# Batch 0 of a spectral filter and MLP kernel: two-bank products and evictions, tables inside the filter stage, filter halves copied within SBUF

## The chip, the cores and the metric

The kernel runs on one NeuronCore of a Trainium2 chip. The metric is the device time of one execution in microseconds (us), as the median of several runs. A profile, taken by the hardware profiler on one more execution, gives the span from the first to the last instruction; its span is some 1.8 us shorter than the device time of the same run. Engines are named as the profile names them: PE is TensorE's matmuls, PEld its weight loads, DVE is VectorE, ACT is ScalarE, POOL is GpSimd, SP is SyncE.

## The reference

```python
def _attn_ref(x, filt_r, filt_i):             # x: (8, 3008, 256)
    X = np.fft.rfft(x, axis=1)
    Y = X * (filt_r + 1j * filt_i)[None]      # filters: (1505, 256)
    return np.fft.irfft(Y, n=x.shape[1], axis=1)

def _moe_ref(x, w_in, w_out):                 # 24064 tokens, 256 -> 2048 -> 256
    h = x @ w_in
    g = 0.5 * h * (1.0 + erf(h / sqrt(2)))    # exact gelu
    return g @ w_out
```

The second function takes the first one's output, all batches in a row. All inputs and the output are float32; the kernel computes in bf16 with float32 sums.

## The kernel before

The Fourier transform of 3008 = 47 x 64 points is done as matmuls with small tables (T1 to T4). For batches 1 to 7 these matmuls are strewn among the MLP matmuls of the batch ahead. Batch 0 has nothing to hide behind: the MLP can't start before all of its output y is there, since its last step writes columns that are spread over the whole sequence. That path, and nothing else, is changed. Its stages are:

```python
    for k, n in ((0, 4), (4, 6), (10, 6), (16, 8)):
        m.load_filters(k, n)      # 4 parts of 8 DMAs: 2 tensors x 4 groups of 32 partitions;
                                  # groups 2 and 3 hold the same data as groups 0 and 1
    m.load_w_in()
    for u in range(16):
        m.c1(u // 2, u % 2)       # first transform of x
        ...
    m.load_x(1); m.load_w_out(0); m.load_w_out(8)
    m.tables_inverse()            # T4 and T3: matmuls, then evictions by DVE and ACT
    for p in range(14):
        if p < 12:
            m.c1t(p)              # transpose, evicted by ACT
        if 1 <= p < 13:
            m.c2(p - 1)           # second transform, times the filter on DVE
        ...
        if p in (3, 5, 7, 9, 11, 13):
            m.c3((p - 3) // 2)    # inverse; evicted by ACT into vt
    for u in range(20):           # last stage
        if u < 16:
            m.c3t(u)              # transposes of vt, evicted into d
        if u >= 3 and u % 2 == 1 and (u - 3) // 2 < 8:
            for h in range(2):
                m.s4(0, (u - 3) // 2, h, both=True)   # products with T4, evicted into y
```

```python
    def c2(self, p):              # before: two products of 512 columns from one PSUM bank each
        for t, o, n in ((p1, 1, 0), (p2, 0, 1)):
            ps = self.bank("ps_c2", True)
            ...                   # 2 matmuls
            nc.vector.tensor_tensor(out=t, in0=ps, op=ALU.mult, in1=self.F[:, n, 2*p:2*p+2, :]...)
```

The evictions of d and y alternate between ACT and DVE. F comes by Pool's DMA queue, which casts float32 to bf16 on the way; the framework lets at most eight of these DMAs be in flight.

## Time and profile before

| before | |
|---|---|
| device time, first three runs | 790.97, 791.30, 792.12 us |
| span of the profiled run | 790.6 us |
| granted TensorE clock | 0.999 |
| PE busy | 762.5 us, 96% |
| first filter product | 19.87 us |
| filter parts complete (0 to 3) | 17.1, 23.3, 29.4, 35.1 us |
| last filter product ends | 39.54 us |
| first MLP matmul (ps_h) | 50.20 us |
| from there to the end | 740.4 us |

The table is to be read from below. The last row is 94% of the span and is TensorE nearly without a gap, so only the 50.2 us above it can move by this change, and they are read from the waits of DVE, ACT and the DMA queue rather than from shares of busy time. The lines follow in the prediction.

### The profile page before, as it was taken

The page shows a single profiled execution, that of the slowest core. Times are in us where ns is not written, and L with a number is a line of the kernel's source. Part 1 is how long each engine was busy: PE and PEld are TensorE (multiplying, and loading weights), DVE is VectorE, ACT ScalarE, POOL GpSimd, SP SyncE. Part 2 cuts the span into 40 slices and gives each one's busy share as a digit, 9 for nine tenths or more (in the row PEclk, how much of TensorE's full clock was granted, in tenths as well). Part 3 has the DMA queues.
Part 4 walks back from the last instruction along what each step waited for, and adds up shares of the span by engine and source line. Part 5 has one row for each costly group of instructions (what it writes and reads, how often), then busy time and mean ns, then how long its engine had stood idle before and what let it go on. Part 6 is the DMA issues. An engine that isn't in the chain of part 4 may idle for free.

```text
span 790.6 us, 14618 instructions
## 1 busy us (share of the span) xinstructions
PE 762.5 (96%) x5817; PEld 539.1 (68%) x5914; DVE 407.6 (52%) x733; ACT 570.5 (72%) x982; POOL 65.3 (8%) x161
## 2 busy tenths in 40 slices
PE   4799999999999999999999999999999999999997
PEld 4556776677676767667677676667767767666666
DVE  7784756466464645646455564546645366411011
ACT  6688965798557885588755887569865688666663
POOL 8610200011000200002000010001100000000000
PEclk9999999999999999999999999999999999999999
DMA  8994862555435553446614566154642521401111
GB/s 128 178 161 132 158 161 68 147 119 114 114 84 155 104 135 84 109 139 130 145 50 109 148 119 157 40 160 108 125 130 65 162 78 58 133 31 38 41 41 54
DMA packets 88390, 87.21 MB, mean 110 GB/s; under 512 B 6081, under 2 KB 78273, under 8 KB 88321
## 3 DMA queue, kind: packets, MB, share of 16 engines
q1 hardware_dynamic: 77760, 68.70, 30.6%
q0 software_dynamic: 10560, 17.57, 15.5%
q8 instruction: 46, 0.75, 0.4%
q14 instruction: 24, 0.19, 0.1%
HBM read 57.15 MB, written 46.66 MB: 131 GB/s over the span
## 4 chain that ended last, share of the span: by engine, by line
PE 90%; DMA 5%; DVE 2%; POOL 1%; issue 1%; ACT 0%; SPq 0%; DVEq 0%; POOLq 0%
PE ps_o L420 41%; PE ps_h L406 37%; PE ps_s L231 3%; PE ps_s L306 3%; PE ps_s L278 2%; PE ps_s L254 2%; DMA d_sb<-R 1%; DMA F<-in_filt_i_dram 1%; DMA F<-in_filt_r_dram 1%; DMA x_sb<-in_x_dram 1%; DVE d_sb L218 1%; POOL x_sb L87 1%; POOL F L95 1%; DMA R<-a_sb 1%; DMA b_sb<-R 0%
## 5 line engine op out<-in xcount | busy, mean ns | idle before, releaser
L409 ACT ACTIVATE g_sb<-ps_h 128x512 bf16<-128x512 f32 x752 | 439.4, 597 | 189.1 <-PE ps_h L406 163.5
L420 PE MATMUL ps_o<-w_out_sb,g_sb 128*128 128x256 bf16 x3008 | 449.0, 272 | 3.0
L406 PE MATMUL ps_h<-y_sb,w_in_sb 128*128 128x512 bf16 (+2 forms) x1503 | 426.6, 365 | 0.2 <-ACT y_sb L216 0.2
L420 PEld LDWEIGHTS <-g_sb 128*128 128x128 bf16 x3008 | 287.6, 98 | 133.7
L406 PEld LDWEIGHTS <-w_in_sb 128*128 128x128 bf16 x1600 | 155.1, 98 | 23.0 <-issue 0.5
L424 DVE COPY ost<-ps_o 128x512 f32<-128x512 f32 x94 | 64.4, 685 | 125.1 <-PE ps_o L420 124.6
L261 DVE TENSOR_TENSOR p<-ps_s,F 128x512 bf16<-128x512 f32 x84 | 58.1, 692 | 103.8 <-ACT p L260 97.3
L220 DVE TENSOR_SCALAR y_sb<-ps_s 128x376 bf16<-128x376 f32 x120 | 65.3, 548 | 82.0 <-PE ps_s L306 81.9
L218 DVE CAST a_sb<-ps_s 96x512 bf16<-96x512 f32 x112 | 76.3, 685 | 40.5 <-PE ps_s L231 40.4
L218 DVE CAST v_sb<-ps_s 128x512 bf16<-128x512 f32 x84 | 57.6, 687 | 12.9 <-PE ps_s L278 12.7
L306 PEld LDWEIGHTS <-d_sb 96*128 96x128 bf16 x512 | 33.8, 97 | 30.2 <-issue 2.3
L259 ACT ACTIVATE p<-ps_s 64x512 bf16<-64x512 f32 x84 | 49.9, 594 | 2.2 <-ACT g_sb L409 0.2
L260 ACT CAST p<-ps_s 64x512 bf16<-64x512 f32 x84 | 48.5, 577 | 1.0
L100 POOL COPY gate<-p 1x1 bf16<-1x1 bf16 x48 | 8.5, 176 | 480.6 <-DVE p L263 480.6
L231 PE MATMUL ps_s<-x_sb,T 94*96 94x512 bf16 x112 | 42.6, 381 | 0.5
L306 PE MATMUL ps_s<-T,d_sb 96*128 96x94 bf16 x448 | 36.3, 204 | 2.6 <-DMA d_sb<-R 1.3
L263 DVE TENSOR_TENSOR p<-p,p 128x512 bf16<-128x512 bf16 x84 | 35.7, 425 | 2.9
L87 POOL DMA_DIRECT2D x_sb<-in_x_dram x64 | 33.9, 530 | 19.0 <-issue 11.1
L262 DVE TENSOR_TENSOR p<-p,F 128x512 bf16<-128x512 bf16 x84 | 34.9, 415 | 0.0
L254 PE MATMUL ps_s<-b_sb,T 128*128 128x256 bf16 x168 | 32.1, 273 | 0.3
L278 PE MATMUL ps_s<-p,T 128*128 128x256 bf16 x168 | 32.1, 273 | 0.3
L278 PEld LDWEIGHTS <-T 128*128 128x128 bf16 x168 | 16.4, 98 | 20.1 <-DVE p L263 0.5
(84 smaller groups left out, 189.0 us busy)
## 6 DMA issues: line engine op xcount, KB each, us to landing
out_dram<-ost SPq DMA_DIRECT2D x94, 256.0 KB, 2.5
x_sb<-in_x_dram POOLq DMA_DIRECT2D x64, 188.0 KB, 3.9
R<-a_sb SPq DMA_DIRECT2D x56, 192.0 KB, 3.0
b_sb<-R SPq DMA_DIRECT2D x28, 384.0 KB, 4.4
R<-v_sb SPq DMA_DIRECT2D x42, 256.0 KB, 4.0
d_sb<-R SPq DMA_DIRECT2D x56, 192.0 KB, 4.6
w_in_sb<-in_moe_w_in_dram POOLq DMA_DIRECT2D x2, 512.0 KB, 8.6
w_out_sb<-in_moe_w_out_dram POOLq DMA_DIRECT2D x2, 512.0 KB, 10.1
```

The costliest lines, as they stand in the source:

```text
L218: self.nc.vector.tensor_copy(out=out, in_=in_)
L220: self.nc.vector.tensor_scalar(out=out, in0=in_, scalar1=scale, scalar2=None, op0=ALU.mult)
L231: nc.tensor.matmul(ps[0:96, :], lhsT=self.T1, rhs=self.st[b, "x"][:, 2 * u:2 * u + 2, :], start=True, stop=True)
L259: nc.scalar.activation(out=p2[0:64], in_=ps[64:128], func=AF.Copy, scale=-1.0)
L260: nc.scalar.copy(out=p2[64:128], in_=ps[0:64])
L261: nc.vector.tensor_tensor(out=p1, in0=ps, in1=f(0), op=ALU.mult)
L278: nc.tensor.matmul(ps[:, 256 * i:256 * i + 256], lhsT=self.T3[:, k].rearrange("p a b -> p (a b)"), rhs=w[:, 256 * i:256 * i + 256], start= ...
L306: nc.tensor.matmul(ps[:, 94 * i:94 * i + 94], lhsT=d[:, (grp % 2) * 4 + i, 128 * half:128 * half + 128], rhs=t4, start=True, stop=True)
L406: nc.tensor.matmul(ps[:, o:o + n], lhsT=self.w_in_sb[:, dc, jc * 128:jc * 128 + 128], rhs=self.ring[:, dc, off:off + n], start=(dc == 0), ...
L409: nc.scalar.activation(out=self.st["g", t][:, jc, :], in_=ps, func=AF.Gelu)
L420: nc.tensor.matmul(ps[:, tile_i % 2, :], lhsT=g[:, jc, tile_i * 128:tile_i * 128 + 128], rhs=self.w_out_sb[:, jc, :], start=(jc == 0), sto ...
L424: nc.vector.tensor_copy(out=ost, in_=ps)
```

## The change

Its intent is a shorter front. A product with the filter covers two PSUM banks (1024 columns) and one DVE instruction instead of two; the transposes and inverses around it work two units ahead on single banks; T3 and T4 are made inside the filter stage instead of ahead of it; d and y are evicted two banks at a time; and of the last three filter parts only one half comes from HBM, the other, which holds the same data, is copied from it within SBUF, so that fewer DMAs with fewer small packets are needed. PSUM is divided into three sets of pools, one after the other.

```diff
-    for k, n in ((0, 4), (4, 6), (10, 6), (16, 8)):
-        m.load_filters(k, n)
+    m.load_filters(0, 4, 2)
+    m.load_filters(4, 6)
+    m.load_filters(10, 6)
+    m.dup_filters(4, 6)
+    m.load_filters(16, 8)
+    m.dup_filters(10, 6)
+    m.dup_filters(16, 8)
     m.load_w_in()
...
+    def dup_filters(self, k0, k):
+        self.nc.gpsimd.dma_start(out=self.F[64:128, :, k0:k0 + k, :], in_=self.F[0:64, :, k0:k0 + k, :])
...
-    m.tables_inverse()
-    for p in range(14):
...
+    for p in range(3):
+        m.c1t(p)
+    for q in range(7):
+        if q < 6:
+            m.c2(2 * q)
+            m.table_3(q)
+            if 2 * q + 3 < 12:
+                m.c1t(2 * q + 3)
+            m.c2(2 * q + 1)
+            if 2 * q + 4 < 12:
+                m.c1t(2 * q + 4)
+        if q == 4:
+            m.table_4()
+        if q >= 1:
+            m.c3(q - 1)
+    wide.close()
+    wide = ctx.enter_context(ExitStack())
+    m.psum(wide, v=(4, 2))
+    for u in range(10):
+        if u < 8:
+            m.c3t(u)              # 8 transposes, one eviction of 1024 columns
+        if u >= 2:
+            m.c4(u - 2)           # 8 products, one eviction of 752 columns
+    wide.close()
+    m.psum(ctx, h=(3, 1), o=(2, 1), f=(3, 1))
...
     # c2
+        ps = self.bank("ps_c2", "w")                 # [128, 2, 512]
         ...
+        nc.vector.tensor_tensor(out=w, in0=ps, op=ALU.mult,
+                                in1=self.F[:, :, 2 * p:2 * p + 2, :]...)
```

Cut: the table routines, the pool bookkeeping, a table load of ACT that comes earlier, and c1, whose first eight evictions are now all ACT's and its last eight all DVE's.

## The prediction

> **What bounds the kernel now.** I read the shares of the span, the chain that ended last in order of time, and then the DVE timeline of the stretch that the chain pointed to.
>
> ```profile
> PE 762.5 (96%) x5817; PEld 539.1 (68%) x5914; DVE 407.6 (52%) x733; ACT 570.5 (72%) x982; POOL 65.3 (8%) x161
> ...
> PE 90%; DMA 5%; DVE 2%; POOL 1%; issue 1%; ACT 0%; SPq 0%; DVEq 0%; POOLq 0%
> ```
>
> TensorE bounds the span: 90% of the chain. The other tenth is nearly all at the front, where batch 0 goes through its transform before the first matmul of the MLP (ps_h). In the chain in order of time (start, duration, what):
>
> ```profile
> 29.64 5.50 DMA F<-in_filt_i_dram
> ...
> 38.86 0.69 DVE p L352
> ...
> 39.97 1.08 ACT vt_sb L370 x2
> 41.05 0.05 issue
> 41.10 0.58 PE ps_c3t L383 x7
> ...
> 45.10 0.46 DVE y_sb L220
> 45.56 0.60 DVE d_sb L218
> ...
> 50.20 0.61 PE ps_h L406 x2
> ```
>
> The first ps_h starts at 50.20; from there the chain is TensorE almost without a break. So the change, which touches batch 0 alone, is worth what it moves that 50.20 by, at most a few per cent of 790.6. Two stretches decide it. Up to 39.55 DVE multiplies with the filters and waits for them:
>
> ```profile
> 19.87 3.08 DVE L352 TENSOR_TENSOR p<-ps_c,F 128x512 bf16<-128x512 f32 x5 [0.58 <-DMA F<-in_filt_r_dram]
> 23.39 3.08 DVE L352 TENSOR_TENSOR p<-ps_c,F 128x512 bf16<-128x512 f32 x5 [0.44 <-DMA F<-in_filt_i_dram]
> 27.03 0.69 DVE L352 TENSOR_TENSOR p<-ps_c,F 128x512 bf16<-128x512 f32 x1 [0.55 <-PE ps_c L349]
> 29.48 3.90 DVE L352 TENSOR_TENSOR p<-ps_c,F 128x512 bf16<-128x512 f32 x6 [1.76 <-DMA F<-in_filt_i_dram]
> 35.26 4.28 DVE L352 TENSOR_TENSOR p<-ps_c,F 128x512 bf16<-128x512 f32 x7 [1.87 <-DMA F<-in_filt_i_dram]
> ```
>
> The brackets are idle time before a group and its releaser: the last seven products start when the last filter part lands (29.64 + 5.50 = 35.14). From 41.10 to 50.20, 9.1 us, DVE goes without a break through d and y, 0.60 + 0.46 = 1.06 us a round, eight rounds; ACT has slack there (7.6 us busy of 9.1).
>
> **What the Trainium skill says.** "DMA: Bandwidth & Descriptors", section "Anatomy of one DMA", gives a DMA about 2.0 us of fixed time, most of it the receipt of the last write. The trace agrees in kind: the quickest filter part landed 2.75 us after its issue began. Section "Two DMAs through the same engine are not ordered" says that the issuing engine must wait for the first DMA's semaphore before it issues one that reads its bytes; the waits in the changed kernel do so: each SBUF copy of the filters stands in Pool's queue behind a wait for the four parts it copies. No copy of that kind is in the trace of before. "ScalarE: Activation LUTs", section "Step-by-step: what each stage is for", has 0.833 ns per element whatever the function; here 595 ns for 512 columns and 486 for 376 give 109/136 = 0.80. "PSUM — Partial Sum Buffer", section "Terms", limits one matmul output to one bank: the wide tiles save no matmul, only instructions of the readers.
>
> **The change part by part.**
>
> *Wide products.* Two DVE products of 512 become one of 1024. Back to back, five took 3.08 us, the last 0.69, so one each 0.60. CAST rows of 687 ns (512 columns) and y rows of 548 ns (376) give 139/136 = 1.02 ns per column, so a wide one takes 0.60 + 512 x 1.02 ns = 1.12. That saves 0.08 per pair, 1 us over twelve, but only the pairs after the last filter wait count.
>
> *Filters.* Before, 32 DMAs, Pool issuing one per 0.53 us and holding eight in flight. After, part 0 (8 DMAs) is as before; the other three parts are loaded into 64 partitions (4 DMAs each) and copied to the other 64 by one DMA each: 23 issues. By the trace's packet records a 512-byte packet of the mirrored loads takes 60 ns, 3072 bytes 248, 4096 bytes 324. Part 1 before is 4 x 32 x 248 + 4 x 192 x 60 ns = 78 us over 16 engines, 4.9 us; half is 2.4. A plain 3072-byte packet (reads of b_sb) took 121 ns, so the copy's 128 packets take about 1.0 us. All four parts: 19.5 us of all engines before, about 3.3 + 8.1 + 3.3 = 14.7 after.
>
> The copies cost latency instead. DMAs 16 to 19 of the queue (part 1's half) have the place of the first four of part 1 before, which landed from 17.5 to 21.6. Pool waits for them (four semaphores), so the copy's issue begins at about 22.0. The four DMAs of part 2's half, issued up to 19.0, stand ahead until 23.3, as before. The copy lands at the later of 22.0 + 2.9 and 23.3 + 1.0 plus some receipt: about 25.0. Before, part 1 was complete at 23.27: **part 1 comes 1.7 us later**. Part 3's loads follow from 22.6 to 24.7, part 2's copy lands near 28, part 3's loads near 27.6, and its copy, issued at 27.9, near 31, against 35.14: **the last part comes 4 us earlier**.
>
> *DVE from the second part on.* After landing at 25.0 DVE has ten wide products (2 to 11), 10 x 1.12 = 11.2; three evictions of T3 at 0.60 that the change puts among them, 1.8; the two small ones of T4, 0.5 together. That is 13.5, so 38.6 without any wait. Product 5 is reached at 25.1 + 3 x 1.12 + 0.6 = 29.1, after 28; product 8 near 33, after 31. So the filter wait that ended the stage before is gone, and DVE itself, started late, takes its place. TensorE and ACT are nearly as full: in a step of two products ACT has four copies at 0.53 and half a T3, 2.4 us; TensorE 2 x 0.44 + 2 x 0.22 + 0.3 + 0.85 = 2.5; DVE 2 x 1.12 + 0.3 = 2.55. Three engines so level, with two wide buffers, will not fit without gaps; I add 0.5. End near 39.1 against 39.55: 0.4 gained.
>
> *Tables inside the stage* leave the front: c1's end to the first product was 15.3 to 19.4. The first product should start near 18.3 instead of 19.87. That gain dies in the wait for part 1's copy.
>
> *Wide evictions of d and y.* Each eviction of d becomes 1024 columns, of y 752. By turns, ACT gets seven d and one y, DVE seven y and one d. ACT: 0.48 between two copies of 512 now, plus 512 x 0.80 ns, 0.89. DVE y: 0.46 + 376 x 1.02 ns = 0.85. TensorE: eight transposes 0.45 and eight products 0.33 to 0.45 a unit. So a unit takes 0.9 instead of 1.06. Filling: 0.45 of transposes, six d in a row on ACT after the first, then for the last unit product 0.45 and y 0.9. Writing the order out with these durations gives 8.35 us from the first transpose to the first ps_h, against 9.1: 0.75 gained. Both pool handovers wait only for evictions that the data need anyway.
>
> *After it.* w_in (issued near 28.4) and the next x need 5.2 + 7.6 us of DMA, so they land by about 43, before 49. Per-slot work behind is unchanged and moves as a block.
>
> Sum: 0.4 + 0.75 = 1.15 us. 791.3 - 1.2 = **790.1**.
>
> **Rivals.** (1) The copies come later or the three level engines jam: 26 instead of 25, and gaps of 1.5 instead of 0.5, would end the products at 41; the time is then 792. For it: Pool waited up to 1.3 us at single filter landings, and the rings are full from 19 us on. Against: the copies carry few, large packets. (2) The copies are quick and the early start carries through: with part 1 complete at 23.5 and no gaps the products end at 37.1, and the first ps_h comes near 47: 788. For it: 4.8 us of DMA work vanish. Against: a wait on a landing plus a second latency cannot be had below 2.75 us after 21.6. (3) The earlier MLP start runs into x(1) or the weights and the gain is lost: 791. In before they landed by 47.5 and 53.1, w_out needed only at 60.6; with less filter work they come earlier still.
>
> **Range and chances.** The terms are 0.4 (plus or minus 1.3), 0.75 (0.5) and the run-to-run spread of about 0.5 (790.97 to 792.12). Range 788.0 to 792.2. Two per cent is 15.8 us, more than any rival gives: faster 0.01, same 0.98, slower 0.01.
>
> **What would show it.** The DVE timeline: the third wide product starts at 24 to 26, waiting for a DMA into F; after it no wait for a filter. The wide product 1.1 to 1.2 us long. The last one ends at 38 to 40; from first c3t transpose to first ps_h 8 to 8.7 us; first ps_h near 49; the rest of the span unchanged to 0.5. I am wrong if products 8 to 11 still wait for a filter, if ACT or TensorE hold DVE for more than 1.5 us in that stage, or if the stretch after the first ps_h changes length.

## The result

The changed kernel took 796.62 us (median of four runs, 795.74 to 798.60) against 791.71 us (790.97 to 792.32) for the kernel before in the same rounds. The ratio is 1.0066, with a 95% interval of 1.0043 to 1.0089: the mean time of the one kernel's fast runs over that of the other's in the same rounds, so not quite the ratio of these medians. The outputs were correct. It is slower by 0.7%, within 2% as the chances said, but 4.4 us above the top of the range.

The first page lines of the changed kernel, as shown of before:

```profile
PE 768.1 (97%) x5914; PEld 540.4 (68%) x5914; DVE 406.5 (51%) x716; ACT 569.1 (72%) x971; POOL 60.7 (8%) x152
...
PE 91%; DMA 2%; ACT 1%; issue 0%; DVE 0%; SPq 0%
```

DVE has 17 instructions fewer and ACT 11, and it bought nothing: neither bounds the span. The shares of the chain don't compare with before's, since the profile could follow this chain back only to 44.22. Its pieces (start, us, what):

```profile
44.22 0.74 issue
44.96 1.03 ACT d_sb L209
...
47.02 4.68 ACT d_sb L209 x5
51.70 0.05 issue
51.75 0.52 PE ps_c L388 x8
52.27 0.02 issue
52.30 0.95 DVE y_sb L213
53.25 0.04 issue
53.29 0.42 PE ps_s L224
53.71 0.43 PE ps_h L411 x2
```

In the timeline the first ps_h starts at 53.54, where it was 50.20. Behind it the two kernels agree: 740.5 us to the end, 740.4 before. So of the 3.5 us between the two spans (794.1 and 790.6), 3.3 were lost ahead of the MLP. Where is seen in DVE's timeline of the products, which answers to the one of before (start, us, instruction, in brackets the idle time before it and its releaser):

```profile
19.55 1.23 DVE L343 TENSOR_TENSOR p<-ps_c,F 128x1024 bf16<-128x1024 f32 x1 [1.83 <-PE ps_c L340]
...
25.38 1.23 DVE L343 TENSOR_TENSOR p<-ps_c,F 128x1024 bf16<-128x1024 f32 x1 [2.91 <-DMA F<-in_filt_r_dram]
26.52 0.68 DVE L211 CAST T<-ps_t 128x512 bf16<-128x512 f32 x1
27.12 2.35 DVE L343 TENSOR_TENSOR p<-ps_c,F 128x1024 bf16<-128x1024 f32 x2
33.00 2.35 DVE L343 TENSOR_TENSOR p<-ps_c,F 128x1024 bf16<-128x1024 f32 x2 [3.53 <-DMA F<-F]
...
41.43 1.21 DVE L343 TENSOR_TENSOR p<-ps_c,F 128x1024 bf16<-128x1024 f32 x1
```

The third product waits for part 1's copy until 25.3, as predicted. The sixth then waits 3.5 us for a second copy, F<-F, which was to be there by 28 and landed at 32.71. From 33.00 DVE works without a wait to 42.64. Pool's timeline has the copies (L93) and the loads (L90) between them:

```profile
21.32 0.62 POOL L93 DMA_DIRECT2D F<-F  x1 [1.39 <-DMA F<-in_filt_i_dram]
...
24.10 0.62 POOL L93 DMA_DIRECT2D F<-F  x1
31.65 0.58 POOL L93 DMA_DIRECT2D F<-F  x1 [6.93 <-DMA F<-in_filt_i_dram]
```

The second copy was issued at 24.10 and took 8.6 us to land; the DMA view of 24.5 to 27 us gives its size and this time:

```profile
F<-F POOLq DMA_DIRECT2D x1, 384.0 KB, 8.6
```

The third stood at the head of Pool's queue for 6.9 us until the loads of part 3, issued from 21.93 to 24.11, had landed, the last at 31.04.

One thing more differs. The granted clock of the changed kernel's four timed runs was 0.997, 0.996, 0.995 and 0.992, and their times 795.8, 795.7, 797.4 and 798.6 us. The trace's clock records show what such a number is made of: in the profiled run a stretch of 3.4 us at half clock, from 28.3 to 31.7, that the trace of the kernel before didn't have (both have one more at the very end).

### The profile page after: what moved, and what is told of

Same layout as the page of the kernel before. It is cut to its first block, busy times and chain, and to the rows that moved or that the text cites. A ratio compares the mean times of both kernels' runs of the same rounds, so it can differ in the third digit from the quotient of the medians.

```text
span 794.1 us, 14666 instructions
## 1 busy us (share of the span) xinstructions
PE 768.1 (97%) x5914; PEld 540.4 (68%) x5914; DVE 406.5 (51%) x716; ACT 569.1 (72%) x971; POOL 60.7 (8%) x152
## 4 chain that ended last, share of the span: by engine, by line
PE 91%; DMA 2%; ACT 1%; issue 0%; DVE 0%; SPq 0%
PE ps_o L425 40%; PE ps_h L411 40%; PE ps_s L224 3%; PE ps_s L297 2%; PE ps_s L272 2%; PE ps_s L247 2%; DMA d_sb<-R 2%; ACT d_sb L209 1%; DMA b_sb<-R 0%; PE ps_c L388 0%; DVE y_sb L213 0%; DVE ost L429 0%; PE ps_c3t L373 0%; SPq L287 0%
## 5 line engine op out<-in xcount | busy, mean ns | idle before, releaser
L411 PE MATMUL ps_h<-y_sb,w_in_sb 128*128 128x512 bf16 (+3 forms) x1600 | 448.0, 367 | 0.0
L213 DVE TENSOR_SCALAR y_sb<-ps_s 128x376 bf16<-128x376 f32 x112 | 61.0, 548 | 82.0 <-PE ps_s L297 82.0
L297 PEld LDWEIGHTS <-d_sb 96*128 96x128 bf16 x448 | 30.3, 97 | 28.3 <-issue 2.4
L257 DVE TENSOR_TENSOR p<-p 128x512 bf16<-128x512 bf16 x84 | 35.7, 425 | 2.9
```

Of the source, the lines that this page charges most:

```text
L213: self.nc.vector.tensor_scalar(out=out, in0=in_, scalar1=scale, scalar2=None, op0=ALU.mult)
L297: nc.tensor.matmul(ps[:, 94 * i:94 * i + 94], lhsT=d[:, (grp % 2) * 4 + i, 128 * half:128 * half + 128], rhs=t4, start=True, stop=True)
L411: nc.tensor.matmul(ps[:, o:o + n], lhsT=self.w_in_sb[:, dc, jc * 128:jc * 128 + 128], rhs=self.ring[:, dc, off:off + n], start=(dc == 0), ...
```

## The experiments

My theory was C: the copies deliver the filters late. Its rivals were W, that the new order of work with its two wide buffers holds the stage whatever the filters do, and K, that the half-clock stretches cost the time. The table holds what the traces of all kernels show (us from the start; landings of parts 1, 2 and 3 complete, the copies included), the median of the timed runs and the median of the kernel before in the same rounds.

| kernel | parts 1, 2, 3 complete | products end | first ps_h | between the two | median | before beside it |
|---|---|---|---|---|---|---|
| before | 23.3, 29.4, 35.1 | 39.54 | 50.20 | 10.66 | | |
| changed | 25.3, 32.7, 35.9 | 42.64 | 53.54 | 10.90 | 796.62 | 791.71 |
| e1 full loads | 23.8, 29.2, 35.3 | 41.09 | 51.99 | 10.90 | 793.50 | 791.51 |
| e2 before, with copies | 26.1, 32.9, 36.5 | 42.05 | 52.72 | 10.67 | 795.70 | 791.51 |
| e3 copies from SyncE | 28.3, 33.4, 38.3 | 44.09 | 55.00 | 10.91 | 798.22 | 791.51 |
| e4 fillers | 26.4, 31.0, 34.8 | 41.44 | 52.34 | 10.90 | 796.79 | 791.51 |
| e5 full loads, tables in front | 23.7, 28.7, 34.8 | 39.59 | 50.68 | 11.09 | 793.84 | 791.44 |
| e6 crosswise copies | 26.1, 30.7, 32.7 | 40.51 | 51.41 | 10.90 | 794.64 | 791.44 |
| e7 narrow evictions | 25.0, 31.3, 34.8 | 41.20 | 52.52 | 11.32 | 795.78 | 791.44 |
| e8 before, other parts and split | 23.8, 29.7, 33.6 | 38.24 | 48.73 | 10.49 | 790.98 | 791.44 |
| e9 split copies, same side | 25.6, 30.3, 32.4 | 40.97 | 53.47 | 12.50 | 795.76 | 791.11 |
| e10 fillers to the end | 26.3, 31.3, 35.1 | 41.35 | 52.49 | 11.14 | 795.77 | 791.11 |
| e11 changed again | 25.8, 32.2, 35.9 | 42.12 | 54.72 | 12.60 | 796.60 | 791.11 |

All gave correct outputs; each experiment was run in five rounds, six timed runs in all. Positions come from one trace of each kernel. The two traces of one and the same program, "changed" and e11, differ by 0.5 us in the end of the products, so a difference of that size between two rows shows little there; the way from there to the first ps_h repeats better (10.90 in four rows).

### e1: no copies

```diff
-    m.load_filters(0, 4, 2)
-    ...                         # halves and copies
+    for k, n in ((0, 4), (4, 6), (10, 6), (16, 8)):
+        m.load_filters(k, n, 2)
```

> The changed kernel with all four quarters of every filter part loaded from HBM, no SBUF copies. Theory C (the copies delay the parts): the parts land as in the kernel before, near 23.3, 29.4 and 35.1 us, DVE waits for the last one, and the first ps_h comes near 51.5 to 52 instead of 53.54, since T3 and T4 evictions now follow among the last products; time near 794 to 795. Theory W (the new order of work and the two wide buffers hold the stage, whatever the filters do): first ps_h stays within 0.5 of 53.5, time 796 to 797.

The first ps_h came at 51.99, inside what theory C said, 1.55 earlier than in the changed kernel; the time fell to 793.5 (ratio to before 1.0027, interval 1.0012 to 1.0042), half a microsecond better than the lower end of what I had expected. C holds for this part. But 1.8 us over the kernel before remain with the same landings as before, so W holds for another part. The lines of the end of this stage:

```profile
35.43 2.36 DVE L343 TENSOR_TENSOR p<-ps_c,F 128x1024 bf16<-128x1024 f32 x2 [1.74 <-PE ps_c L356]
37.70 0.32 DVE L192 TENSOR_SCALAR T<-ps_t,wt 96x94 bf16<-96x94 f32 x1
37.92 0.32 DVE L192 TENSOR_SCALAR T4c<-ps_t,wtc 96x94 bf16<-96x94 f32 x1
38.14 1.21 DVE L343 TENSOR_TENSOR p<-ps_c,F 128x1024 bf16<-128x1024 f32 x1
39.27 0.68 DVE L211 CAST T<-ps_t 128x512 bf16<-128x512 f32 x1
39.87 1.22 DVE L343 TENSOR_TENSOR p<-ps_c,F 128x1024 bf16<-128x1024 f32 x1
```

The wait in the first line is put down to PE, but the last filter part landed at 35.31, just before, so it was the DMA. From there to the end of the products are 5.78 us; in the kernel before, 39.54 - 35.14 = 4.40. Between the products stand table evictions, which here are on the path: 0.44 (T4) and 0.60 (T3), counted from start to next start.

### e2: the kernel before with the copies

```diff
 # the kernel before
-    for k, n in ((0, 4), (4, 6), (10, 6), (16, 8)):
-        m.load_filters(k, n)
+    m.load_filters(0, 4, 2); m.load_filters(4, 6); m.load_filters(10, 6); m.dup_filters(4, 6)
+    m.load_filters(16, 8); m.dup_filters(10, 6); m.dup_filters(16, 8)
```

> The kernel before with only the filter loading of the changed one. Theory C: part 2's copy lands near 32 to 33 and its last near 36, the products end near 41 instead of 39.55, first ps_h near 51.5 to 52; time 793 to 794. Theory W: within 0.5 us of the kernel before.

Part 2's copy landed at 32.86 and the last at 36.45, as C said. The first ps_h came at 52.72 and the time was 795.7, both worse than I expected (52 and 794): fourteen narrow products were left, and they ran from 32.98 to 42.05. So the loading alone, in an otherwise untouched kernel, costs 2.5 us at the first ps_h; W's "within 0.5 us" is refuted. The ratio was 1.0047 (1.0034 to 1.0061).

### e3: copies from SyncE

```diff
-        self.nc.gpsimd.dma_start(out=self.F[64:128, ...
+        self.nc.sync.dma_start(out=self.F[64:128, ...     # each right after its part's loads
```

> The changed kernel, the three copies issued from SyncE, each right after its part is loaded, so Pool never waits for a landing. Theory C1 (what hurts is Pool's queue held up by the waits and the copies' places in it): part 1 complete near 23, part 2 near 26.5, part 3 near 30; DVE waits only for part 1; the products end near 37 to 38 and the first ps_h comes near 48 to 48.5; time 789 to 790. Theory C2 (a copy within SBUF from 64 partitions to the other 64 is itself slow and slows the loads beside it): copies still take 4 us and more and the last part lands after 33; first ps_h 51 or later.

It is the slowest of all. Pool no longer waits for a landing, yet the copies landed 7.3, 8.9 and 8.6 us after their issue and the parts were complete at 28.3, 33.4 and 38.3. Pool now ran ahead: it issued w_in from 22.1 on, where the changed kernel did from 32.2, and those transfers share the engines with the filters: 324 ns for each packet of 4096 bytes. From 25 to 30 us 139 such packets started on Pool's queue, of which part 3's loads can be 64 at most. The expectation under C1 fell, and C2 is what happened, though w_in mixes into it. The copies' own packets were not slow here: 3072 bytes in 134 ns (median), close to the 121 ns of the prediction. In the changed kernel Pool's wait, unintended, had kept w_in behind the filters.

### e4: fillers

```diff
+    def filler(self, n):
+        ps = self.bank("ps_fill", "n")
+        for i in range(n):
+            self.nc.tensor.matmul(ps, lhsT=self.eye, rhs=self.T2[:, 0:8, 1, :], start=True, stop=True)
...
+            if q in (2, 3):
+                m.filler(10 if q == 2 else 6)
             m.c2(2 * q)
```

> The changed kernel with 10 and 6 matmuls of 512 columns that nobody reads, put where TensorE waits for DVE's third and fifth product. Theory K (part of the loss is the lower granted clock that follows the new idle stretches of TensorE; in the four timed runs of the changed kernel each further 0.003 of clock goes with 1.5 us): the granted clock is 0.999 in all runs, no half-clock stretch at 28 us, the time falls to 794.5 to 795.5 with a spread under 1 us, first ps_h still near 53.5. If the clock plays no part: 796 to 797 as before.

The stretch at 28 us was gone from the trace, but another stood there from 52.6 to 56.1, at the MLP's start, and the timed runs had clocks of 0.995 to 0.999 and a median of 796.79, although part 2's copy happened to land earlier and the first ps_h came 1.2 us before the changed kernel's. Theory K as I had put it failed. The trace told why: the stretch at 28 us lies in DVE's wait for the filter and costs nothing that can be seen. The one at the MLP's start does. From the first ps_h to the start of the sixteenth gelu the kernel before took 10.42 us and the changed one 10.44, this run 12.08.

### e5: full loads, tables in front

```diff
 # e1
+    m.table_4()
+    for q in range(6):
+        m.table_3(q)
     for p in range(3):
         m.c1t(p)
...
-            m.table_3(q)
-        if q == 4:
-            m.table_4()
```

> The run with full loads, with the tables T3 and T4 made before the stage as in the kernel before; what is left of the change is then the wide products, the order two units ahead and the wide evictions. Theory T (the table evictions among the last products, 0.6 + 0.5 us of DVE, are most of what e1 still loses): products end near 40.0 instead of 41.09, first ps_h near 50.9, time near 792.3, 1 us under e1. Rival (two wide PSUM buffers hold DVE): products still end at 40.8 or later.

The products ended at 39.59 and the first ps_h came at 50.68, 1.3 before e1 and 0.5 behind the kernel before. Some of that is luck with the landing (34.76 against 35.31). Counted from the landing, 39.59 - 34.76 = 4.83 us, 0.95 less than e1: the tables on the path, as theory T said; the rival, that two wide buffers hold DVE to 40.8 or later, fell. The rest, 4.83 against 4.40, goes with the wide product:

```profile
34.88 4.71 DVE L343 TENSOR_TENSOR p<-ps_c,F 128x1024 bf16<-128x1024 f32 x4 [2.61 <-DMA F<-in_filt_i_dram]
```

Four wide products are left when the imaginary half lands; the kernel before had done the first real product of the part by then and had seven narrow ones left, in 4.28 us. The median, 793.84, was worse than expected (792.3), but its six runs go from 791.8 at a clock of 1.000 to 796.8 at 0.993. The one run at 1.000 is close to the kernel before (median 791.44); a single run shows no more.

### e6: crosswise copies

```diff
-            for q, a in enumerate(...[:2 * halves]):
-                nc.gpsimd.dma_start(out=self.F[32 * q:32 * q + 32, t, ...], in_=a)
+                r = 32 * q + (64 * t if halves == 1 else 0)
+                nc.gpsimd.dma_start(out=self.F[r:r + 32, t, ...], in_=a)
...
+        for t in range(2):
+            src, dst = 64 * t, 64 - 64 * t
+            self.nc.gpsimd.dma_start(out=self.F[dst:dst + 64, t, ...], in_=self.F[src:src + 64, t, ...])
```

The thought was the Trainium skill's "SBUF — State Buffer", section "Door 1: The DMA port swizzle", which has partitions 0 to 63 reached through only half of the DMA ports.

> The changed kernel, but of the later parts the real half is loaded into partitions 0 to 63 and the imaginary half into 64 to 127, and the copies go crosswise, two DMAs a part; the same bytes. Theory S (the Trainium skill's SBUF page: partitions 0 to 63 are reached through only half of the DMA ports, so the loads and the copies' reads of the changed kernel crowd on one half, their writes on the other): part 3's loads land by 28.5 instead of 31.04, part 2's copy by 30 instead of 32.71, the last copy by 33, first ps_h near 51.5; time near 794.5. Rival (the copies cost DMA engine time and a second latency wherever they lie): part 2's copy again after 32, first ps_h 53 to 54, time 796 to 797.

The result is near theory S and far from its rival: part 3's loads landed at 29.30 and part 2's copy at 30.73 (each 0.7 to 0.8 later than S said), the last at 32.70, first ps_h 51.41, time 794.64 (ratio 1.0036, interval 1.0021 to 1.0051). Yet the edit does two things: it spreads over both halves, and it cuts each copy in two, which can be issued as soon as their own two loads are there. Hence e9.

### e9: split copies, same side

```diff
-        self.nc.gpsimd.dma_start(out=self.F[64:128, :, ...], in_=self.F[0:64, :, ...])
+        for t in range(2):
+            self.nc.gpsimd.dma_start(out=self.F[64:128, t, ...], in_=self.F[0:64, t, ...])
```

> Control for the crosswise copies: the changed kernel with each copy cut in two DMAs, one for the real and one for the imaginary half as in e6, but all from partitions 0 to 63 to 64 to 127 as in the changed kernel. Theory S (it is the crowding on one half of the partitions that e6 took away): part 3's loads land at 30 to 31, part 2's copy complete after 31.5, the last after 34.5, products end 41.5 to 42.7, first ps_h 52.5 to 53.5; time 795.5 to 796.6. Rival (it is the earlier issue of smaller copies): as e6, 30.7 and 32.7, first ps_h near 51.4, time near 794.6.

Part 3's loads landed at 28.40, part 2's copy at 30.28 and the last at 32.36, as early as in e6 or earlier. Theory S fell; what e6 gained came from the cut. The whole copies of six traces (the changed kernel, e2, e4, e7, e10, e11) completed part 2 at 30.95 to 32.86 and part 3 at 34.75 to 36.45, the two with split copies at 30.28 and 30.73, and 32.36 and 32.70. The DMA view of one and the same window, 24.5 to 27 us, in the kernel before, the changed one and e9 (packets, MB, mean rate):

```profile
DMA packets 470, 0.37 MB, mean 150 GB/s; under 512 B 61, under 2 KB 408, under 8 KB 470
```

```profile
DMA packets 284, 0.28 MB, mean 112 GB/s; under 512 B 38, under 2 KB 241, under 8 KB 284
```

```profile
DMA packets 530, 0.43 MB, mean 170 GB/s; under 512 B 51, under 2 KB 483, under 8 KB 530
```

With the whole copy the engines move less in this stretch, right behind the first copy, than they did with the full loads; with e9's split copies they move more (with e6's 143 GB/s, about as much). This window is picked, though: from 22 to 29.5 us as a whole the rates are 154 (before), 164 (changed), 215 (e9) and 197 GB/s (e6). So the changed kernel moves no less than the kernel before; the split copies move more than either. Part of the cause is the issue: in e9 the first half copy went out at 19.82 and the loads of part 3 from 21.47 on, in the changed kernel at 21.32 and from 21.93 on. Whether that is all, or whether a whole copy also loads the 16 engines unevenly, these runs don't show; the second would fit that in the changed kernel the engines were busy for only 23% from 29.5 to 32 us, while the last loads of part 3 and part 2's copy were still landing. Nor do they show whether a single copy from 64 partitions to the other 64 has a limit of its own, since e6 and e9 both consist of such copies. In time e9 gained less (795.76): besides one at 28.5 its trace has half-clock stretches at 42.2 and 52.4, and 12.5 us instead of 10.9 between the products and the first ps_h.

### e7: narrow evictions

```diff
-    m.psum(wide, v=(4, 2))
-    for u in range(10):            # c3t and c4, 1024 and 752 columns
+    m.psum(wide, v=(8, 1))
+    for u in range(20):            # c3t and s4 of the kernel before, 512 and 376 columns
```

> The changed kernel with d and y evicted from single banks as in the kernel before, alternately by ACT and DVE. Theory N (wide evictions gain nothing: ACT's 512-column copies cost 0.48 us each back to back, half of the 0.95 us of a wide one, and the longer pieces lengthen the first and the last step): from the first c3t transpose to the first ps_h 9.1 to 9.3 as with the wide ones, 9.28; time within 0.3 of the changed kernel. My prediction's claim, that wide ones save 0.75 us, would make it 10.0 and the time 0.8 longer.

It came out between the two. From the end of the products to the first ps_h this kernel took 11.32 us, the changed one 10.90, the kernel before 10.66. So the wide evictions are worth 0.42 us inside the changed kernel, where I had predicted 0.75 and theory N nothing, and what stands around them costs 11.32 - 10.66 = 0.66. ACT's lines of the last stage, first of the kernel before, then of the changed one:

```profile
39.97 1.07 ACT L370 CAST vt_sb<-ps_c 128x512 bf16<-128x512 f32 x2 [1.32 <-PE ps_c L366]
41.48 1.08 ACT L216 ACTIVATE d_sb<-ps_c3t 96x512 bf16<-96x512 f32 x2 [0.43 <-PE ps_c3t L383]
```

```profile
43.13 1.07 ACT L360 CAST vt_sb<-ps_c 128x512 bf16<-128x512 f32 x2 [1.58 <-PE ps_c L356]
44.96 6.74 ACT L209 ACTIVATE d_sb<-ps_c3t 96x1024 bf16<-96x1024 f32 x7 [0.75 <-ACT vt_sb L360]
```

Seven wide evictions take 6.74 us; after the first of 1.03 (the chain above) that is 5.71 / 6 = 0.95 each. Two narrow ones end to end took 1.08, the first start to the second 1.08 - 0.59 = 0.49. A wide one is thus hardly cheaper than two narrow ones (0.95 against 2 x 0.49): narrow ones back to back overlap by 0.10 us. The narrow stage has its first eviction of d 1.94 us after the last product (41.48 - 39.54), the wide one 2.32 (44.96 - 42.64). And in the kernel before the first s1 matmul of the next batch (its first transform, into ps_s) ran at 49.63, ahead of the last y; in the changed one its bank belongs to the pool of y, so it waits for the last y and delays the first ps_h by 0.25 us (53.29 to 53.54).

### e10 and e11: the clock

```diff
 # e4
             m.c4(u - 2)
+        if u >= 8:
+            m.filler(1 if u == 8 else 4, "v")
```

> The kernel with the fillers of e4 and five more matmuls that nobody reads: one before the last y product and four before the first MLP matmul, where TensorE waits about 0.4 and 1.0 us for an eviction. Theory K2 (a half-clock stretch that begins at the MLP's start costs 1.7 us, 12.1 instead of 10.4 to the 16th gelu; one before it, while DVE waits for a filter, costs nothing, so e4 gained nothing): granted clock 0.998 to 1.000 in nearly all runs, spread of the runs under 1.5 us, median 0.8 to 1.5 us under the changed kernel run beside it. If the clock of the timed runs does not matter: same median as beside it.

e11 is the changed kernel without any edit.

> The changed kernel once more, for a second trace and six more times with their granted clocks, beside e9 and e10. Theory: part 2's copy lands 8 us and more after its issue again, DVE waits over 2 us for it, products end 41.5 to 42.7; the runs with a granted clock of 0.996 or less are 1 to 3 us longer than those above. If the late copy was an accident of one trace, the products end near 39.5 and the first ps_h near 50.5.

The changed kernel gave the same again: part 2's copy 7.7 us after its issue (a little under the 8 I had named), a wait of 2.53 us for it, products to 42.12. This time the trace caught the half-clock stretches where they hurt. PE busy and the granted clock (the last but two columns) in four windows of e11, then in the first three of them of e10:

```profile
43.60:47.00 3.40, 3.26 (x34) 3.26 (x34) 1.22 (x1) 1.61 (x3) 2.11 (x4) 0.50 1.06 208
50.40:53.80 3.40, 2.00 (x35) 1.52 (x31) 2.94 (x4) 2.53 (x4) 0.00 (x0) 1.00 1.44 195
53.80:57.20 3.40, 3.13 (x7) 1.32 (x9) 1.47 (x3) 1.12 (x2) 0.00 (x0) 0.50 0.22 31
57.20:60.60 3.40, 3.40 (x17) 1.67 (x16) 3.30 (x6) 2.78 (x6) 0.00 (x0) 1.00 0.30 61
```

```profile
43.60:47.00 3.40, 3.13 (x60) 2.86 (x58) 2.89 (x4) 3.20 (x4) 1.69 (x3) 1.00 1.07 211
50.40:53.80 3.40, 3.07 (x20) 1.52 (x22) 2.42 (x5) 1.53 (x3) 0.00 (x0) 1.00 1.26 169
53.80:57.20 3.40, 3.40 (x17) 1.71 (x16) 3.40 (x7) 3.12 (x6) 0.00 (x0) 1.00 0.38 74
```

In e11 PE is busy for 2.00 of the 3.4 us from 50.4, and in the next 3.4 us it runs at 0.50 and starts 7 matmuls; a window later, at full clock, 17. The same befell it at 43.6, after a window from 40.1 with PE busy for 1.49 of 3.5 us. But a wait of TensorE is not always followed by half clock: after e11's window from 29.9 to 33.3 (busy 1.56 us) and e6's from 26.5 to 29.9 (1.70) the clock stayed at 1.00. In e10 PE is busy for 3.07 us in the window with the same numbers, and the clock stays at 1.00. The stretch at 43.6 lengthens e11's way from the products to the first ps_h to 12.60 from 10.90; the other costs 1.0 us by the sixteenth gelu (11.42 against 10.44).

The ten timed runs of the changed kernel (first four and e11's six) have a clock of 0.992 to 0.997, and each 0.001 less goes with 0.71 us more (a straight line through them, correlation -0.92 between clock and time). The 33 timed runs of the kernel before beside the experiments give nearly the same, 0.69 us, with a correlation of -0.74. As for the expectation: e10's clocks were 0.997 to 0.999 and its median 0.83 under e11's, as said, but its spread was 2.5 us and not 1.5. The medians of e10 and e11 lie inside each other's ranges, so by time alone the fillers are not shown to help.

### e8: an attempt at a better kernel

```diff
 # the kernel before
-    for k, n in ((0, 4), (4, 6), (10, 6), (16, 8)):
+    for k, n in ((0, 4), (4, 6), (10, 8), (18, 6)):
...
 # c3t
-        self._evac(d[...], ps[0:96, :], True)
+        self._evac(d[...], ps[0:96, :], False if u == 1 else "act")
 # s4 of batch 0
-        self._evac(yv, pv, both, 1.0 / self.S)
+        self._evac(yv, pv, "act" if both and grp == 7 and half == 1 else False, 1.0 / self.S)
```

> The kernel before with two small changes, an attempt at a better one: the filter parts hold 4, 6, 8 and 6 columns instead of 4, 6, 6 and 8, so that after the last landing five products are left instead of seven; and in the last stage ACT evicts d and DVE y, but for one of each, still from single banks. From the spacing of 0.60 us per product the products end 1.2 us earlier, near 38.3; the last stage is 8.5 to 8.7 us instead of 9.1; first ps_h near 48.5; time near 789.8, 1.7 under the kernel before. If the filter DMAs, and not the products after them, set the end, only the half microsecond of the last stage is gained.

The products ended at 38.24 and the first ps_h came at 48.73, both close to what was said. From the products to the first ps_h it is 10.49, 0.17 better than before where I had hoped for 0.5. DVE's last groups:

```profile
29.77 4.50 DVE L352 TENSOR_TENSOR p<-ps_c,F 128x512 bf16<-128x512 f32 x7 [1.45 <-DMA F<-in_filt_i_dram]
34.48 3.76 DVE L352 TENSOR_TENSOR p<-ps_c,F 128x512 bf16<-128x512 f32 x6 [0.21 <-PE ps_c L349]
```

The last filter wait is gone: part 3 landed at 33.62 while DVE still worked on part 2. The time was 790.98 (790.57 to 791.12, all six runs at a clock of 0.999 or 1.000) against 791.44 (789.81 to 793.21); ratio 0.9992, interval 0.9980 to 1.0004. Its trace is 1.5 us ahead of the one trace of the kernel before, but the kernel before beside it had runs of 789.81 and 790.49 too. So it is the steadiest of all and perhaps half a microsecond faster; that it beats the kernel before is not shown.

## Why the prediction was wrong

The prediction had the first part of the story right (a late first copy, then DVE as the limit), but said that no later product waits for a filter and that the last stage gains. Both failed, and with them the sign of the sum.

**The copies.** "Part 2's copy lands near 28, part 3's loads near 27.6, and its copy, issued at 27.9, near 31" is the step that failed. Measured were 32.71, 31.04, 31.65 and 35.93. Part 1's copy, at 25.30, was right. So were part 2's loads, at 23.40. From there on the prediction spread all packets evenly over 16 engines: 1.0 us for the first copy, 3.2 for part 3's loads (by its packet times), 1.0 for the second copy, 5.2 together. By the packet records they took 1.7, 4.05 and 1.1 us of all engines, 6.9 together. So 1.7 of the 4.7 us by which the second copy was late are longer packets, in the first copy (6144 bytes in a median of 474 ns, 483 in e11) and in the loads; in the second copy they took 247 ns, about twice the 121 ns that the prediction assumed for 3072. The other 3.0 us go with engines that were not kept busy: their share from 23.0 to 31.2 us was 79%, against 115% in the kernel before from 27.0 to 35.2 and 109% in e9 from 23.0 to 28.5 (over 100%, since records of packets overlap). The copy that came late was thus not slow itself; its packets started only between 27.40 and 31.40, among those of part 3's loads, and it was its wait behind them that was mis-sized. "Product 5 is reached at 29.1, after 28" therefore became a wait of 3.53 us. Taking the copies away (e1) gives 1.55 us back at the first ps_h; putting them alone into the kernel before (e2) costs 2.5. Rival 1 named the danger, and gave it 792 at most.

**The DVE sum.** Its terms were right: 1.12 us a product was predicted, and from 33.00 to 42.64 are seven products, two T3 and the T4 pair, 7 x 1.12 + 1.2 + 0.5 = 9.5 against 9.64 measured. The gaps among the three level engines, for which I added 0.5 us, didn't occur behind the copy. What I did not draw from it is that the tables' 0.95 us (e1 against e5), done ahead of the filters in the kernel before, now stood behind the last filter wait; and that a wide product must wait for both halves of the filter, which goes with 0.43 (e5). Set end to end, the delay of the first ps_h is 1.55 (copies, e1) + 0.95 (tables) + 0.43 (wide products) + 0.17 (e1's last part landed at 35.31, the kernel before's at 35.14) + 0.24 (last stage) = 3.34 us, each from single traces.

**The last stage.** "0.75 gained" was 0.24 lost, counted from the end of the products (from the first transpose of vt, as the prediction counted, 9.28 us came instead of 8.35). The prediction also misread the kernel before: DVE's unbroken run starts at 41.70, not at 41.10, so 0.6 of its 9.1 us was a fill already. Wide evictions save 0.42 (e7). The terms that failed are ACT's 0.89 a wide eviction, measured 0.95; the fill, which made the first eviction 0.38 later than before; and "both pool handovers wait only for evictions that the data need anyway": the s1 matmul needed only a bank, waited for the last y, and put 0.25 us in front of the MLP.

**The clock.** The prediction had no word on it. The traces show stretches of 3.4 us at half clock; those of e11 follow windows in which TensorE was busy for 1.49 of 3.5 and 2.00 of 3.4 us, though not every such window has one behind it. The one at 28 us, in DVE's wait, cost nothing that can be seen. One in the last stage or at the MLP's start went with 1.0 to 1.7 us (e4, e11). The medians are 4.9 us apart and the profiled pair of spans 3.5. Of the rest, 0.8 is that the changed kernel's profiled run (795.84) lies under its median, and 0.7 that the one of before (792.37) lies over its own. That the clock makes the changed kernel's runs scatter, and some of its median, is a correlation and a few traces, not an experiment that took the clock alone away: e10, which tried, was faster by an unresolved 0.8.

**What was right.** Nothing behind the first ps_h changed (740.53 and 740.40). The change stayed within 2%. The first product came earlier, and this gain died in the wait for part 1's copy, though the product was at 19.55 and not 18.3. Rival 3, that the weights come late, didn't occur.

**What stays open.** Why one copy of 64 partitions with both halves, and the loads behind it, land later than two copies of one half each, and why the engines stood partly idle meanwhile. That spreading over both halves is what helped in e6 fell to its control (e9); the earlier issue explains some of it. What share of a window TensorE may wait before half clock follows is open too.

## What to carry to other kernels

A transfer that depends on another transfer is read as two latencies in a row plus the queue ahead of the second, and packet times summed over 16 engines don't tell how long that queue takes (its engines were 79% busy here, 115% in the kernel before); a load that repeats bytes may be cheaper than a copy that waits. Work that moves out of a busy front into a stage should be placed ahead of that stage's last arrival, since everything behind it is on the path. Wider instructions gain little where the narrow ones are already back to back, as on ACT here, and pools that hand over memory between stages can order work that the data leave free.

## What the Trainium skill lacked or had wrong

- "TensorE: Matmul & The Clock Gate", section "Part 1: The HAM clock gate", says that the clock halves after an idle window of about 3.4 us and that the window is free-running. The length agrees: 3.41 us for the stretch at 28.3 in the changed kernel. But here the window before was not idle throughout: TensorE was busy for 2.00 of 3.4 us (e11, from 50.4) and the next stretch ran at 0.50. What share of a window has to be busy is on no page, and the runs give no limit either (2.00 was followed by half clock, 1.56 and 1.70 elsewhere were not).
- "DMA: Bandwidth & Descriptors", section "Anatomy of one DMA": by its formula, 2.0 us plus bytes over 436 GB/s, I estimate 2.9 us for a copy of 384 KB by itself. In the changed kernel, with other DMAs in flight, it took 4.0 us (first copy) and 8.6 us (second, behind four loads of one 32-partition group each). The page has no measured figure for a copy within SBUF on this queue; the packets of 6144 bytes took a median of 474 ns in the first copy and 247 in the second.
- "ScalarE: Activation LUTs" lacks nothing here, though I had passed it over: its section "What ACT_TABLE_LOAD costs" says that back-to-back ACTIVATEs overlap by about 93 ns. The runs agree: 0.59 - 0.49 = 0.10 us for evictions of 512 columns, 1.03 - 0.95 = 0.08 us for 1024. So one of 1024 columns costs nearly as much as two of 512.
